# A fused transformer block: the second gate/up starts with twelve half tiles, one norm is transposed by DMA, and one chunk's Q, K, V become paired matmuls

## The chip, the cores and the metric

The kernel runs on one core of a Trainium2 chip. The metric is the device time of one execution in microseconds (us); the number compared is the median of several executions. The profile comes from one further execution that was taken with the hardware profiler.

## What is computed

The input x has 2048 rows of 576 values in bf16. A small matrix product of silu(c) with w_mod gives six vectors of 576: shift, scale and gate for each of two halves.

```python
h = layernorm(x) * (1 + ca) + sa
x = x + ga * attention(h)          # 32 heads of 18, each row attends to 8 rows: itself and 2, 4, .. 14 back
h = layernorm(x) * (1 + cb) + sb
x = x + gb * ((h @ w_gate) * (h @ w_up)) @ w_down      # 576 -> 4608 -> 576
```

## The kernel before

The rows are cut into eight chunks of 256 (two tiles of 128 rows each), and the chunks into five groups for the second half: [0], [1, 2], [3, 4], [5, 6], [7]. For each group the kernel runs a gate/up stage (`gate_up`: 36 column tiles of 128, each the product of gate and up) and then a down stage (`down`: 36 row tiles accumulated into PSUM). The attention of later chunks is cut into small pieces that are put between the tiles of these stages, so that TensorE always has matmuls to run.

The contraction over 576 is four and a half times 128. A *pair* (class `Pair`) runs two matmuls at once, one on rows 0 to 63 of the array and one on rows 64 to 127, so that the half step costs half; the tail of the operand must then be present in both halves of the partitions (`both` in the norms writes it twice, `both_halves` and `wo_both` copy it for the weights). The *full* form pads the half step to 128 rows. Before the change, chunks 0, 1, 2 and 4 use the full form for Q, K, V (`a_q`, `a_v`) and chunks 3, 5, 6 and 7 use pairs (`qkv_of`); the output projection is a pair for chunks 3, 5 and 7 (`wo_of`) and full for the others (`b_w`).

A normalised chunk must be transposed before it can be multiplied. Either TensorE does it through PSUM (`transposed`, used by `a_t` and `b_t`; the modulation then reads PSUM), or the DMA does it from SBUF to SBUF (`a_td`, `b_td`, issued on SP; the modulation `a_mod` or `b_mod` then works in place). `b_o` transposes the attention output o_sb to oT on TensorE, `b_od` by DMA.

**The order.** All engines run in the order in which the program issues instructions. `timed` makes that order: it walks the tiles of a stage with a clock of assumed costs, and after each tile takes pieces from several threads. A piece is a tuple (TensorE us, VectorE us, the marks it needs, the mark it makes, the wait until that mark counts, the call). Pairs come from a list of their own (`extra`), at most one before each tile, in order. What did not fit in a gate/up stage goes to the down stage behind it (`among`, `first_down`), and what did not fit there is the `left` of the next gate/up.

**The second gate/up** (group [1, 2]) can begin on chunk 1 alone: `gate_items` starts it with `HEAD` = 8 half tiles for chunk 1 ("f0", 256 columns), then the same 8 for chunk 2 ("f1", which need the mark h2), then whole tiles of 512 columns. Weights for gate and up (`load_wgu`, on SP) come in blocks of four tiles into three buffers, so block 3 can only be asked for when block 0 has been used by both chunks: at the fifth f1 tile. W_down (`load_wd`) and the values of attention (`b_ld`, 1.1 MB each) are loaded on GpSimd's queue.

**Chunk 2 before the change**: its values are weighted and summed in the first down stage, its output projected (`b_o`, `b_w`), its second norm (`b_ln`, `b_norm`) finished at the start of the second gate/up and transposed by TensorE there (`b_t(2)`). Chunk 4's norm is transposed by TensorE (`a_t4`) at the start of the first down stage, and its Q, K, V follow there in the full form. Chunk 1's output projection is there too.

Of the kernel before, what the change touches and what calls it, by code (L numbers as in the profile page):

```python
# [39 lines left out]
GC = D // 4  # L40

GROUPS = [[0], [1, 2], [3, 4], [5, 6], [7]]
PAIRED = (3, 5, 7)


@with_exitstack
def kernel(
# [279 lines left out]
    def transposed(src, dst, cols, vi):  # L327
        n = P * len(cols)
        pA = ps([P, 3, n], BF, "tr_pA")
        pB = ps([P, 2, n], BF, "tr_pB")  # L330
        for m in range(KT):
            d = pA[:, m, :] if m < 3 else pB[:, m - 3, :]
            for c, j in enumerate(cols):
                nc.tensor.transpose(d[:, js(c)], src[:, j, m * P:(m + 1) * P], ident[:])

        def evict(first_on_dve=True):
            for m in range(KT):
                s = pA[:, m, :] if m < 3 else pB[:, m - 3, :]
                modulate(dst(m), s, m, vi + 1, vi, (m < 3) == first_on_dve)
        return evict  # L340

    def mod_columns(wm, pi, fill=lambda: None, steps={}, order=(KF, 0, 1, 2, 3)):
# [49 lines left out]

    def a_ln(i):
        x = x_in.pop(i)
        xn, rsq, norm = layernorm(lambda j: x[:, j, :], "a", i in (3, 4), i in (3, 5, 6, 7))
        aa[i] = dict(xn=xn, rsq=rsq, norm=norm)

    def a_norm(i):
# [21 lines left out]
            nc.sync.dma_start_transpose(out=aa[i]["hT"][:, :, js(j)], in_=aa[i]["xn"][:, j, :])  # L420

    def a_t4():
        a_t(4, False)
        nc.gpsimd.memset(aa[4]["hT"][64:, KF, :], 0.0)

    def a_mod(i, ms, on_dve=True):
        hT = aa[i]["hT"]
# [47 lines left out]
    def b_ld(i, j):  # L475
        b = bb.setdefault(i, dict(prod={}, vsh={}))
        base = HALO + i * CH + j * P - DIL * (W - 1)
        vsh = vshp.tile([P, W, DH, H], BF, name="vsh")
        vsrc = bass.AP(vd.tensor, vd.offset + base * D, [[D, P], [DIL * D, W], [1, D]])
        b["vsh"][j] = vsh  # L480
        return nc.gpsimd.dma_start(vsh[:].rearrange("p w d h -> p w (d h)"), vsrc)  # L481

    def b_p(i, w):
        b = bb.setdefault(i, dict(prod={}, vsh={}))
# [197 lines left out]
        transposed(bb.pop(i)["xn"], lambda m: ht[:, m, o0:o0 + CH], (0, 1), 2)()  # L682


    def b_td(i):
        ht, o0 = h2_of(i)
        xn = bb.pop(i)["xn"]
        for j in range(ST):
            nc.sync.dma_start_transpose(out=ht[:, :, o0 + j * P:o0 + (j + 1) * P], in_=xn[:, j, :])

    def b_mod(i, ms, on_dve):
        ht, o0 = h2_of(i)
# [32 lines left out]
    def values_of(i, nxt=None):  # L725
        r = []
        for j in range(ST):
            r += [(0, 0.75, f"a{i}", "-", 0, lambda j=j, w=w: b_mul(i, j, w)) for w in range(0, W, 2)]
            r += [(0, 0.75, "", "-", 0, lambda j=j: b_add(i, j, 0)), (0, 0.75, "", "-", 0, lambda j=j: b_add(i, j, 1)),
                  (0, 1.2, "", f"o{i}{j}", 0, lambda j=j: b_add(i, j, 2))]  # L730
            if i in PAIRED:
                r.append((0, 0, "", f"O{i}" if j == ST - 1 else "-", 11.0 if i == 7 else 14.0, lambda j=j: b_od(i, (j,))))
            if nxt is not None:

                r.append((0, 0, f"v{nxt}", "-", 0, lambda j=j: behind(b_ld(nxt, j), bb[i]["od"]) if (i, j) == (3, 1) else b_ld(nxt, j)))
        return r
# [153 lines left out]

    QKP = [(0, 1), (2, 3), (4,), (5, 6), (7, 8)]

    def timed(items, extra, threads, slack, busy=0.0):

        t, dve = 0.0, busy
        done, seq = {f"v{i}": 0.0 for g in GROUPS for i in g[1:]}, []
        done["late"] = 0.0
        extra, threads = list(extra), [list(th) for th in threads]

        def ready(need):  # L900
            return all(done.get(x, 1e9) <= t for x in need.split())

        def fill():
            nonlocal t, dve
            moved = True
            while moved:
                moved = False
                for th in threads:
                    if th and ready(th[0][2]) and (not th[0][1] or dve <= t + slack):
                        pe, d, _, mark, wait, call = th.pop(0)  # L910
                        t += pe
                        dve = max(dve, t) + d if d else dve
                        done[mark] = (dve if d else t) + wait
                        seq.append(("piece", call))
                        moved = True
                        break
        for kind, f, step, own, need in items:
            if seq and extra and ready(extra[0][1]):
                pe, _, mark, make, *ve = extra.pop(0)
                seq.append(("pair", make))  # L920
                t += pe
                dve = max(dve, t) + sum(ve)
# [7 lines left out]
        assert not extra, (extra[0][1], t)  # L930
        return seq, [(*p[0:2], p[2] if all(x in names(th) for x in p[2].split()) else "late", *p[3:]) for th in threads for p in th]

    def names(th):
        return [p[3] for p in th]
# [7 lines left out]
                at[f].append(x)  # L942
        return at, late

    HEAD = 2 * FB

    def gate_items(gi):
        n = len(GROUPS[gi])
# [37 lines left out]
    def wgu_spaces():  # L986
        for k, space in ((3, value_space()), (4, value_space()), (8, prod_t)):
# [1 line left out]
        load_wgu((NG - 1) * NBLK + 3)  # L989
        load_wgu((NG - 1) * NBLK + 4)  # L990

    WD_ASKS = [{0: (7,), 1: (8,), 2: (9,), 7: (10,)},
# [339 lines left out]
    def ld_prods(gi):  # L1332
        for k in range(2):
            g = gi * NBLK + (5 if gi == 0 else 3) + k
            wd_home[g] = prod_t[:, k * FB * D:(k + 1) * FB * D].rearrange("p (k d) -> p k d", d=D)
            r = load_wd(g)
            if gi:
                behind(r, wgu_in[gi * NBLK + NBLK - 1])

    loads = {(0, 23): lambda: behind(load_wd(1), bb[2]["ltd"]), (0, 24): lambda: ld_d1(4), (0, 25): lambda: load_wd(2), **{(gi, 32): lambda gi=gi: ld_prods(gi) for gi in (1, 2, 3)}, (3, 34): wgu_spaces, (NG - 1, 28): lambda: [ld_spare(k) for k in range(4)]}  # L1340

# [18 lines left out]
    at = [k for k, p in enumerate(first) if p[3] == "o11"][0] + 2  # L1360
    first.insert(at, (0, 0, "o11", "O1", 0, nop))
    gbg = {0: (qkv_of(3, "p17 z3"),
               [[(0, 0, "", "-", 0, lambda: (load_wm5(), load_wd(0))), (0, 0, "", "z3", 8.0, nop), (0, 0, "", "w5", 12.0, nop), (0.85, 0, "w5", "-", 0, gb_row), (0, 0, "", "-", 0, lambda: (load_res(2), both_halves()))],
                norm_of(3, "", "", 5) + [(0, 2.5, "", "m4", 0.2, lambda: a_ln(4)), (0, 0, "m4", "r4", 1.0, lambda: aa[4]["rsq"]()),
                                         (0, 0, "r4", "e4", 2.0, lambda: aa[4]["norm"]((0,))), (0, 0, "e4", "n4", 1.6, lambda: aa[4]["norm"]((1,))),
                                         (0, 0, "n4 v3", "x4", 0, nop)],
               first, [(0, 0, "y1", "s1", 0.6, lambda: b_exp(1))]]),
           1: (qkv_of(5, "p37") + wo_of(3),
               [[(0, 0, "", "-", 0, lambda: (loads_v(3), load_res(3), load_res(4), wo_both()))], norm_of(5, "p33", "", 7), second]),
           2: (qkv_of(6, "") + wo_of(5),  # L1370
               [[(0, 0, "", "h6", 1.0, lambda: (loads_v(5), load_res(5), load_res(6)))], attention_of(5, 6)]),
           3: (qkv_of(7, "") + wo_of(7), [[(0, 0, "", "h7", 1.0, lambda: load_res(7)), (0, 0, "v7", "-", 0, lambda: loads_v(7))], [(0, 0, "q74", "-", 0, nop)] + prods_of(7) + softmax_of(7) + values_of(7)]),
           4: ([], [])}

    def first_down(late):
        def q(g):
            return (0.53 if g == 2 else 1.07, 0, "h4", "-", 0, lambda: a_q(4, g))

        def v(j):
            return (1.2, 0, "h4", "-", 0, lambda: a_v(4, j))  # L1380

        def out_1(first):
            return [(0, 0, "", "o0", 0.4, nop), (0.55, 0, "o0", "o1", 1.9, lambda: b_o(1)), (1.2, 1.35, "o1", "-", 0, lambda: b_w(1, 0)), (1.2, 1.35, "", "x1", 0.5, lambda: b_w(1, 1)),
                    (0, 2.5, "", "s1", 0.7, lambda: b_ln(1)), (0, 0, "s1", "n1", 2.3, lambda: b_norm(1)), (0, 0, "n1", "t1", 9.5, lambda: b_td(1)),
                    (0, 1.0, "t1", "-", 0, lambda: (b_mod(1, (3, 4), False), b_mod(1, (0, 1, 2), True)))]
        assert not {"O1", "x4"} & set(names(late))
        a4 = [(0.6, 0, "", "h4", 1.7, lambda: (a_t4(), load_x(6), ld_prods(0)))]
# [19 lines left out]
    for gi, grp in enumerate(GROUPS):  # L1407
# [13 lines left out]
        if gi == NG - 1:  # L1421
            down_last(gi, hh)
        else:
            left = down(gi, hh, first_down(late) if gi == 0 else next_down(gi, late))
            assert gi == 0 or not left


# [28 lines left out]
```

## Time and profile before

| | us |
|---|---|
| three executions | 539.7, 540.89, 541.5 (median 540.89) |
| the profiled execution | 541.99 |
| its span, first to last instruction | 539.7 |
| first gate/up (49.3 to 95.8) | 46.5 |
| first down (95.8 to 127.6) | 31.8 |
| second gate/up (127.6 to 210.1) | 82.5 |

In those three stages TensorE is busy for 46.45, 31.49 and 82.50 us, VectorE for 38.6, 22.8 and 64.7, ScalarE for 34.7, 14.0 and 48.0. The granted TensorE clock is 1.00 throughout. PE is TensorE, DVE VectorE, ACT ScalarE, POOL GpSimd, SP the engine that issues most DMAs. In a group of instructions, "x25" is their number; in a timeline the first two columns are start and duration, and brackets hold the idle time before the instruction and what ended it.

### The profile page before, as it was taken

Reading aid. Unit: us, or ns where it says so; the run is one execution under the profiler, and the core shown is the slowest. Engines: PE = TensorE matmul, PEld = TensorE weight load, DVE = VectorE, ACT = ScalarE, POOL = GpSimd, SP = SyncE. Lnnn points to the kernel's source line nnn. Section 1 sums busy time; section 2 is a strip of 40 time slices with the busy share of each in tenths; the row PEclk is TensorE's granted clock in tenths of the full one; section 3 lists DMA queues with packets and bytes.
Section 4 is the critical chain, followed back from the end, with each engine's and each line's share of the span. In section 5 each row is a group of like instructions: output and inputs, shape, how many; then the busy total and the mean of one; then the engine's idle time right before and its main releaser. Section 6 shows DMA issues by size and latency. Waiting matters only on the chain.

```text
span 539.7 us, 14692 instructions
## 1 busy us (share of the span) xinstructions
PE 531.5 (98%) x6214; PEld 324.0 (60%) x6244; DVE 319.5 (59%) x731; ACT 252.8 (47%) x620; POOL 73.1 (14%) x113
## 2 busy tenths in 40 slices
PE   8999999999999999999999999999999999999997
PEld 4777889756755444555544454555544454558875
DVE  5898797759767788627467797504517733032212
ACT  4866877644656553112655543104555542006630
POOL 8104023112000110111000010110010101110210
PEclk9999999999999999999999999999999999999999
DMA  9999999979863871998445944983396694759731
GB/s 273 292 242 363 346 278 321 322 128 326 279 181 90 237 229 28 264 273 299 130 130 145 302 149 108 238 237 111 94 279 184 158 312 81 233 138 292 259 96 38
DMA packets 94659, 114.47 MB, mean 212 GB/s; under 512 B 27873, under 2 KB 83378, under 8 KB 94466
## 3 DMA queue, kind: packets, MB, share of 16 engines
q1 hardware_dynamic: 82864, 66.92, 45.7%
q0 software_dynamic: 11424, 46.40, 27.5%
q8 instruction: 49, 0.80, 0.7%
q10 hardware_dynamic: 306, 0.21, 0.1%
q14 instruction: 16, 0.13, 0.1%
HBM read 103.07 MB, written 4.74 MB: 200 GB/s over the span
## 4 chain that ended last, share of the span: by engine, by line
PE 97%; DMA 1%; issue 1%; DVE 0%; SPq 0%; ACT 0%
PE pg L770 29%; PE pu L770 23%; PE acc L1007 19%; PE pq L442 4%; PE pq L770 3%; PE accr L1012 3%; PE acc L1062 3%; PE pv L770 2%; PE pv L465 2%; PE lgT L499 2%; PE pw L659 2%; DMA wmA<-in_w_mod_dram 1%; PE pw L770 1%; PE po L614 1%; PE pwj L636 0%
## 5 line engine op out<-in xcount | busy, mean ns | idle before, releaser
L770 PE MATMUL pg<-h2T,wgu 64*128 64x512 bf16 (+1 forms) x1376 | 266.0, 331 | 0.0
L770 PE MATMUL pu<-h2T,wgu 64*128 64x512 bf16 (+1 forms) x1376 | 265.5, 331 | 0.0
L770 PEld LDWEIGHTS <-wgu 64*128 64x128 bf16 x2752 | 136.5, 94 | 93.3
L821 ACT CAST u_sb<-pu 128x512 bf16<-128x512 f32 (+1 forms) x172 | 85.4, 497 | 152.4 <-PE pg L770 150.4
L824 DVE TENSOR_TENSOR hh<-g_sb,u_sb 128x512 bf16<-128x512 bf16 x136 | 59.2, 435 | 114.1 <-ACT g_sb L822 113.1
L822 ACT CAST g_sb<-pg 128x512 bf16<-128x512 f32 (+1 forms) x172 | 86.8, 505 | 0.0
L1007 PEld LDWEIGHTS <-hh 128*128 128x128 bf16 x504 | 49.0, 98 | 59.3 <-issue 1.5
L1007 PE MATMUL acc<-wd,hh 128*128 128x512 bf16 x327 | 84.1, 380 | 0.1
L1012 PE MATMUL accr<-wd,hh 128*128 128x64 bf16 x344 | 62.4, 193 | 0.8
L770 PE MATMUL pu<-h2T,wgr 64*128 64x512 bf16 (+1 forms) x188 | 61.4, 327 | 0.0
L770 PE MATMUL pg<-h2T,wgr 64*128 64x512 bf16 (+1 forms) x188 | 61.4, 327 | 0.0
L1012 PEld LDWEIGHTS <-hh 128*128 128x128 bf16 x504 | 45.8, 98 | 1.2
L175 POOL DMA_DIRECT2D wd<-in_B_w_down_dram x29 | 21.8, 751 | 176.2 <-PE accr L1012 142.0
L548 DVE TENSOR_TENSOR vsh<-vsh,attn 128x1152 bf16<-128x1152 bf16 x56 | 39.7, 750 | 0.0
L487 DVE TENSOR_TENSOR prod_t<-qT,kT 128x1280 bf16<-128x1280 bf16 x36 | 28.2, 817 | 4.5 <-ACT kT L841 2.7
L770 PEld LDWEIGHTS <-wgr 64*128 64x128 bf16 x376 | 19.6, 94 | 15.1 <-issue 2.7
L1007 PE MATMUL acc<-prod_t,hh 128*128 128x512 bf16 x108 | 27.7, 380 | 0.0
L481 POOL DMA_DIRECT2D vsh<-vd x14 | 12.5, 896 | 96.6 <-DVE o_sb L556 76.1
L770 PE MATMUL pq<-hT,wqk 64*128 64x256 bf16 (+1 forms) x360 | 22.9, 259 | 0.0
L442 PE MATMUL pq<-hT,wqk 128*128 128x256 bf16 (+1 forms) x225 | 21.7, 251 | 0.1
L1012 PE MATMUL accr<-prod_t,hh 128*128 128x64 bf16 x112 | 21.6, 193 | 0.2
L325 ACT ACTIVATE h2T<-h2T,modc 128x256 bf16<-128x256 bf16 x12 | 6.5, 591 | 31.4 <-DMA h2T<-xn 31.4
(225 smaller groups left out, 628.3 us busy)
## 6 DMA issues: line engine op xcount, KB each, us to landing
wgu<-in_B_w_gate_dram SPq DMA_DIRECT2D x41, 512.0 KB, 4.8
wgu<-in_B_w_up_dram SPq DMA_DIRECT2D x41, 512.0 KB, 6.5
wd<-in_B_w_down_dram POOLq DMA_DIRECT2D x29, 576.0 KB, 5.2
vsh<-vd POOLq DMA_DIRECT2D x14, 1152.0 KB, 8.8
prod_t<-in_B_w_down_dram POOLq DMA_DIRECT2D x8, 576.0 KB, 5.9
hh<-in_B_w_down_dram POOLq DMA_DIRECT2D x6, 576.0 KB, 6.8
x_t<-in_A_x_dram SPq DMA_DIRECT2D x8, 288.0 KB, 5.3
x_r<-in_A_x_dram SPq DMA_DIRECT2D x8, 288.0 KB, 8.5
```

The lines of the kernel that those rows point to most:

```text
L175: return nc.gpsimd.dma_start(wb[:], B_w_down[r0:r0 + FB * P, :].rearrange("(k p) n -> p k n", p=P))
L442: nc.tensor.matmul(pq[:, gi, :], lhsT=wqk[:, kt, m * P:(m + 1) * P], rhs=hT[:, kt, cols], start=(kt == order[0] and not (by_k and gi)), st ...
L481: return nc.gpsimd.dma_start(vsh[:].rearrange("p w d h -> p w (d h)"), vsrc)
L487: nc.vector.tensor_tensor(prod, aa[i]["qT"][:], aa[i]["kT"][:, :, off:off + CH], ALU.mult)
L548: nc.vector.tensor_tensor(v, v, at, ALU.mult)
L770: return nc.tensor.matmul(out, lhsT=lhs, rhs=rhs, start=first, stop=last, skip_group_check=True)
L821: nc.scalar.copy(u[:, c, :], pu)
L822: nc.scalar.copy(g[:, c, :], pg)
L824: return lambda: nc.vector.tensor_tensor(hh[:, f - c:f + 1, :], g, u, ALU.mult)
L1007: nc.tensor.matmul(acc[j][:], lhsT=hh[:, f, js(j)], rhs=wb[:, f % FB, 0:512], start=(f == 0), stop=(f == FT - 1))
L1012: nc.tensor.matmul(accr[:, j, :], lhsT=hh[:, f, js(j)], rhs=wb[:, f % FB, 512:D], start=(f == 0 and j == 0), stop=(f == FT - 1), skip_grou ...
L1062: nc.tensor.matmul(acc[i][:], lhsT=hh[:, f, js(j)], rhs=wb(f)[:, c0:c1], start=(f == 0), stop=(f == FT - 1))
```

## The change

- `HEAD` becomes 12: the second gate/up begins with twelve half tiles of chunk 1, then twelve of chunk 2.
- Chunk 2's second norm is transposed by DMA (`b_td(2)` and `b_mod(2, ..)` in place of `b_t(2)`). The reads of chunk 3's values wait until that transpose has landed and until h2 in the program; the residual loads of chunks 3 and 4 move with them in the program's order.
- Chunk 4's Q, K, V become pairs: the five for Q and K at the end of the first gate/up, the two for V at the start of the second. Its norm writes its tail twice; its transposes on TensorE move from the first down stage into the first gate/up, and their eviction is all on VectorE. The load of chunk 6's input moves with them.
- Chunk 1's output projection becomes two pairs in the first gate/up; `b_o(1)` moves there, its tail columns of o_sb are filled, and `wo_both` is issued earlier. Chunk 1's second norm is modulated by VectorE alone.
- Chunk 2's weighted values are held back in the planner until 52.5 and 56.5 on its clock (marks V2 and W2).
- `timed` may place pairs after the last tile. W_down's loads in the first down stage are asked for at other tiles, and blocks 5 and 6 wait for chunk 2's first value read.

```diff
-PAIRED = (3, 5, 7)
+PAIRED = (1, 3, 5, 7)
...
-                modulate(dst(m), s, m, vi + 1, vi, (m < 3) == first_on_dve)
+                modulate(dst(m), s, m, vi + 1, vi, first_on_dve == 5 or (m < 3) == first_on_dve)
...
-        xn, rsq, norm = layernorm(lambda j: x[:, j, :], "a", i in (3, 4), i in (3, 5, 6, 7))
+        xn, rsq, norm = layernorm(lambda j: x[:, j, :], "a", i in (3, 4), i >= 3)
...
     def a_t4():
-        a_t(4, False)
-        nc.gpsimd.memset(aa[4]["hT"][64:, KF, :], 0.0)
+        a_t(4, 5)
+        load_x(6)
...
-            if i in PAIRED:
+            if i in PAIRED[1:]:
...
+        for pe, need, mark, make, *_ in extra:
+            assert ready(need), (need, t)
+            seq.append(("pair", make))
+            t += pe
+            done[mark] = t + pe + 1.0
+            fill()
...
-    HEAD = 2 * FB
+    HEAD = 3 * FB
...
-    WD_ASKS = [{0: (7,), 1: (8,), 2: (9,), 7: (10,)},
+    WD_ASKS = [{0: (7,), 3: (8,), 5: (9,), 7: (10,)},
...
-            if gi:
-                behind(r, wgu_in[gi * NBLK + NBLK - 1])
+            behind(r, wgu_in[gi * NBLK + NBLK - 1] if gi else bb[2]["ld"])
...
-    first = attention_of(1, 2)[12:-14]
+    first = attention_of(1, 2)[12:]
+    first.insert(-14, (0, 0, "V2", "-", 0, nop))
+    first.insert(-7, (0, 0, "W2", "-", 0, nop))
...
-    gbg = {0: (qkv_of(3, "p17 z3"),
+    gbg = {0: (qkv_of(3, "p17 z3") + wo_of(1) + qkv_of(4, "p27")[:5],
...
+               [(0, 2.5, "W11", "S1", 0.7, lambda: b_ln(1)), (0, 0, "S1", "N1", 2.3, lambda: b_norm(1)), (0, 0, "N1", "T1", 9.5, lambda: b_td(1)),
+                       (0, 1.7, "T1", "-", 0, lambda: b_mod(1, (3, 4, 0, 1, 2), True))],
+               first, [(1.15, 0, "o11 n4 v3", "O1", 2.3, lambda: (a_t4(), b_o(1))), (0, 0, "O1", "h4", 0.6, nop)],
+               [(0, 0, "y1", "s1", 0.6, lambda: b_exp(1))], [(0, 0, "", "V2", 52.5, nop)], [(0, 0, "", "W2", 56.5, nop)]]),
-           1: (qkv_of(5, "p37") + wo_of(3),
-               [[(0, 0, "", "-", 0, lambda: (loads_v(3), load_res(3), load_res(4), wo_both()))], norm_of(5, "p33", "", 7), second]),
+           1: (qkv_of(4, "")[5:] + qkv_of(5, "p37") + wo_of(3),
+               [[(0, 0, "", "h4", 0, nop), (0, 0, "h2", "-", 0, lambda: (load_res(3), load_res(4), behind(b_ld(3, 0), tds[2]), b_ld(3, 1)))], norm_of(5, "p33 M2", "v4", 7), second]),
...
-              (0, 2.2, "", "s2", 0.7, lambda: b_ln(2)), (0, 1.5, "s2", "n2", 0.2, lambda: b_norm(2)), (0.55, 1.0, "n2", "-", 0, lambda: b_t(2))]
-        return [a4, out_1(True), late + [(0, 0, "", "a2", 0.0, nop)] + values_of(2) + o2, [q(0), q(1), q(2), q(3), q(4), v(0), v(1)]]
+              (0, 2.2, "", "s2", 0.7, lambda: b_ln(2)), (0, 1.5, "s2", "n2", 0.2, lambda: b_norm(2)), (0, 0, "n2", "T2", 6.0, lambda: b_td(2)),
+              (0, 0, "T2", "M2", 0, lambda: (b_mod(2, (3, 4), False), b_mod(2, (0, 1, 2), True)))]
+        return [[(0, 0, "", "-", 0, lambda: ld_prods(0))]] + parts[:-1] + [parts[-1] + o2]
```

More of the change, by code (lines that the diff above doesn't have):

```diff
@@ L480, in b_ld @@
         b["vsh"][j] = vsh
-        return nc.gpsimd.dma_start(vsh[:].rearrange("p w d h -> p w (d h)"), vsrc)
+        r = nc.gpsimd.dma_start(vsh[:].rearrange("p w d h -> p w (d h)"), vsrc)
+        b.setdefault("ld", r)
+        return r
     def b_p(i, w):
@@ L682, in b_t @@
         transposed(bb.pop(i)["xn"], lambda m: ht[:, m, o0:o0 + CH], (0, 1), 2)()
+    tds = {}
     def b_td(i):
@@ L688, in b_td @@
         for j in range(ST):
-            nc.sync.dma_start_transpose(out=ht[:, :, o0 + j * P:o0 + (j + 1) * P], in_=xn[:, j, :])
+            tds[i] = nc.sync.dma_start_transpose(out=ht[:, :, o0 + j * P:o0 + (j + 1) * P], in_=xn[:, j, :])
     def b_mod(i, ms, on_dve):
@@ L891 @@
     QKP = [(0, 1), (2, 3), (4,), (5, 6), (7, 8)]
+    parts = []
     def timed(items, extra, threads, slack, busy=0.0):
@@ L897, in timed @@
         done["late"] = 0.0
+        for x in extra:
+            done.pop(x[2], None)
         extra, threads = list(extra), [list(th) for th in threads]
@@ L929, in timed @@
             t += step
-        assert not extra, (extra[0][1], t)
-        return seq, [(*p[0:2], p[2] if all(x in names(th) for x in p[2].split()) else "late", *p[3:]) for th in threads for p in th]
+        for pe, need, mark, make, *_ in extra:
[4 more added lines that the diff above has]
+            fill()
+        parts[:] = [[(*p[0:2], p[2] if all(x in names(th) for x in p[2].split()) else "late", *p[3:]) for p in th] for th in threads]
+        return seq, [p for th in parts for p in th]
     def names(th):
@@ L1359 @@
     first.pop(at)
-    at = [k for k, p in enumerate(first) if p[3] == "o11"][0] + 2
-    first.insert(at, (0, 0, "o11", "O1", 0, nop))
-    gbg = {0: (qkv_of(3, "p17 z3"),
-               [[(0, 0, "", "-", 0, lambda: (load_wm5(), load_wd(0))), (0, 0, "", "z3", 8.0, nop), (0, 0, "", "w5", 12.0, nop), (0.85, 0, "w5", "-", 0, gb_row), (0, 0, "", "-", 0, lambda: (load_res(2), both_halves()))],
+    gbg = {0: (qkv_of(3, "p17 z3") + wo_of(1) + qkv_of(4, "p27")[:5],
+               [[(0, 0, "", "-", 0, lambda: (load_wm5(), load_wd(0))), (0, 0, "", "z3", 8.0, nop), (0, 0, "", "w5", 12.0, nop), (0.85, 0, "w5", "-", 0, gb_row), (0, 0, "", "-", 0, lambda: (load_res(2), both_halves(), wo_both()))],
                 norm_of(3, "", "", 5) + [(0, 2.5, "", "m4", 0.2, lambda: a_ln(4)), (0, 0, "m4", "r4", 1.0, lambda: aa[4]["rsq"]()),
-                                         (0, 0, "r4", "e4", 2.0, lambda: aa[4]["norm"]((0,))), (0, 0, "e4", "n4", 1.6, lambda: aa[4]["norm"]((1,))),
-                                         (0, 0, "n4 v3", "x4", 0, nop)],
-               first, [(0, 0, "y1", "s1", 0.6, lambda: b_exp(1))]]),
-           1: (qkv_of(5, "p37") + wo_of(3),
-               [[(0, 0, "", "-", 0, lambda: (loads_v(3), load_res(3), load_res(4), wo_both()))], norm_of(5, "p33", "", 7), second]),
+                                         (0, 0, "r4", "e4", 2.0, lambda: aa[4]["norm"]((0,))), (0, 0, "e4", "n4", 1.6, lambda: aa[4]["norm"]((1,)))],
+               [(0, 2.5, "W11", "S1", 0.7, lambda: b_ln(1)), (0, 0, "S1", "N1", 2.3, lambda: b_norm(1)), (0, 0, "N1", "T1", 9.5, lambda: b_td(1)),
[4 more added lines that the diff above has]
+               [[(0, 0, "", "h4", 0, nop), (0, 0, "h2", "-", 0, lambda: (load_res(3), load_res(4), behind(b_ld(3, 0), tds[2]), b_ld(3, 1)))], norm_of(5, "p33 M2", "v4", 7), second]),
            2: (qkv_of(6, "") + wo_of(5),
@@ L1373, with first_down @@
            4: ([], [])}
[L1375 to L1387, printed above, removed]
+    def first_down(parts):
         o2 = [(0, 0, "o21", "z2", 0.6, nop), (0.55, 0, "z2", "O2", 1.1, lambda: b_o(2)), (1.2, 1.35, "O2", "-", 0, lambda: b_w(2, 0)), (1.2, 1.35, "", "x2", 0.2, lambda: b_w(2, 1)),
-              (0, 2.2, "", "s2", 0.7, lambda: b_ln(2)), (0, 1.5, "s2", "n2", 0.2, lambda: b_norm(2)), (0.55, 1.0, "n2", "-", 0, lambda: b_t(2))]
-        return [a4, out_1(True), late + [(0, 0, "", "a2", 0.0, nop)] + values_of(2) + o2, [q(0), q(1), q(2), q(3), q(4), v(0), v(1)]]
+              (0, 2.2, "", "s2", 0.7, lambda: b_ln(2)), (0, 1.5, "s2", "n2", 0.2, lambda: b_norm(2)), (0, 0, "n2", "T2", 6.0, lambda: b_td(2)),
+              (0, 0, "T2", "M2", 0, lambda: (b_mod(2, (3, 4), False), b_mod(2, (0, 1, 2), True)))]
+        return [[(0, 0, "", "-", 0, lambda: ld_prods(0))]] + parts[:-1] + [parts[-1] + o2]
     def norm2_of(i, need):
@@ L1423 @@
         else:
-            left = down(gi, hh, first_down(late) if gi == 0 else next_down(gi, late))
+            left = down(gi, hh, first_down([th for k, th in enumerate(parts) if th and k != 3] + [parts[3]]) if gi == 0 else next_down(gi, late))
             assert gi == 0 or not left
```

## The prediction

> **What bounds the kernel now.** I read the page first, then the waits of the engines, then TensorE's timeline around the edits. The page's busy shares and its chain agree:
>
> ```profile
> span 539.7 us, 14692 instructions
> ...
> PE 531.5 (98%) x6214; PEld 324.0 (60%) x6244; DVE 319.5 (59%) x731; ACT 252.8 (47%) x620; POOL 73.1 (14%) x113
> ...
> PE 97%; DMA 1%; issue 1%; DVE 0%; SPq 0%; ACT 0%
> ```
>
> The chain that ended last is TensorE for 97% of the span. All of TensorE's waits in the whole run, from the view of waits:
>
> ```profile
> PE busy L203 <- DVE busy_w L198: 1.3, 1, 1.3
> PE pv L465 <- issue: 1.1, 1, 1.1
> PE pm L348 <- DMA wmA<-in_w_mod_dram: 0.5, 1, 0.5
> PE pm_t L355 <- PE pm L348: 0.2, 1, 0.2
> ```
>
> All four lie in the prologue, before the first gate/up. (Matmul ends are modelled, so I also compared starts: apart from steps where one record is missing, they show some 1.05 us of delay after 49 us, 0.88 of it at chunk 3's Q, which the change leaves in place.) So the edits are worth the TensorE time that they remove, less any wait that they make. Removed work can bring little; a new wait can cost without limit.
>
> **The change, part by part.** TensorE first, from its timeline:
>
> ```profile
> 103.65 2.89 PE L442 MATMUL pq<-hT,wqk 128*128 128x256 bf16 x25
> 106.38 1.23 PE L465 MATMUL pv<-wv,hT 128*128 128x504 bf16 x5
> 107.44 0.33 PE L467 MATMUL pvr<-wv,hT 128*128 128x72 bf16 x5
> 107.60 1.23 PE L465 MATMUL pv<-wv,hT 128*128 128x504 bf16 x5
> ...
> 132.19 0.51 PE L334 MATMUL tr_pA<-shifts,xn 128*128 128x128 bf16 x6
> 132.54 0.39 PE L334 MATMUL tr_pB<-shifts,xn 128*128 128x128 bf16 x4
> 132.86 0.28 PE L770 MATMUL pg<-h2T,wgr 64*128 64x256 bf16 x1
> ```
>
> and from the chain, pieces of the paired form (chunk 5, chunk 3) beside the full form:
>
> ```profile
> 100.41 1.08 PE pw L659 x5
> ...
> 160.81 0.98 PE pq L770 x18
> ...
> 176.34 1.10 PE pv L770 x18
> ...
> 199.91 1.10 PE pw L770 x18
> ```
>
> Ends overlap the next start, so I take start to start.
>
> 1. *Chunk 4's Q, K, V as pairs.* Now: Q and K are 45 matmuls at 2.73/25 = 0.109 us, 4.91; V is 106.38 to 108.82, 2.44 (the next start). Together 7.35. As pairs: four at 0.98, the half-width one 0.50, two V pairs at 1.10: 6.62. Gain 0.73.
> 2. *Chunk 1's output projection as pairs.* Now 1.08 + 0.15 to 0.21 per tile, 2.51 for two; then 2 x 1.10 = 2.20. Gain 0.31.
> 3. *Chunk 2's second norm by DMA.* Ten transposes leave TensorE: 132.19 to 132.86, 0.67.
> 4. *Twelve half tiles.* Four more tiles cost 2 x 0.982 in place of 1.942 (pitch of half and of full tiles in this stage): +0.09.
> 5. *Chunk 4's and chunk 1's transposes* move from the down stage into the first gate/up. There a change between 64-row and 128-row matmuls costs 0.09 going in and 0.10 coming out (the last half-tile start at 131.99 to 132.19 is 0.20 where the pitch is 0.11): +0.19.
>
> Sum: -0.73 - 0.31 - 0.67 + 0.09 + 0.19 = -1.43 us.
>
> The small edits off TensorE I cost at nothing while TensorE covers them: two more 64-column normalisations on ScalarE for chunk 4, tail adds and memsets of o_sb on VectorE, five modulations moved from ScalarE to VectorE (0.34 each), the copy of wo's tail moved earlier on GpSimd, the memset of hT removed there. VectorE and ScalarE are busy 39 and 35 of 46.5 us in that gate/up; with the cover gone they cost their own 1 to 2 us. The moved loads of W_down I cost at nothing too: blocks 5 and 6 now follow chunk 2's first value read (landed at 97.5), take about 6 us and are needed at down tile 20, 10 us into a stage that starts at 103.8; blocks 7 and 8 start when blocks 0 and 1 are used up, 12 us or more before their tiles, and loads here took 5 to 10. Chunk 6's input is asked a few places earlier on SP and needed far later.
>
> **The waits that it adds.** I walked the planner's rule with the new costs to get the order, and put measured durations on it. The order is unchanged up to tile 32 of the first gate/up (92.4 us). That stage then gains 7.9 us (0.56 + 0.56 + 0.19 + 2.20 + 4.42) and ends at 103.8 instead of 95.85; the first down stage loses 11.0 (7.35 + 2.51 + 2 x 0.56) and ends at 124.6 instead of 127.6.
>
> *PSUM after the moved transposes.* Four banks go through 20 transposes in the middle of the gate tiles; VectorE must drain chunk 4's (5 x 0.34 = 1.7 us, behind the softmax of chunk 2) before two tiles later uses them. Bounds 0 and 0.9; I take 0.2, since the drained banks are due only 1.1 us after the transposes end, about when the first three are drained.
>
> *Chunk 1's transpose and VectorE.* It is issued at about 109, and all five modulations now stand in VectorE's queue ahead of chunk 2's two residual sums, its statistics, and the output of the down stage, which frees the accumulators. How long it takes to land, from the view of tile h2T and the group by line:
>
> ```profile
> L689 SPq DMA_TRANSPOSE h2T<-xn x2: 1200/1251/1302, 111.6 to 112.9; - x2
> ...
> DMA to landing us min/median/max: 7.6/8.9/10.2
> ```
>
> Landing at 119, modulated at 120.5; sums 2.7, statistics 2.0, first accumulators read by 126.9. TensorE asks for those banks at about 127.4. Margin 0.5 us; bounds 0 and 2; I take 0.2.
>
> *Chunk 2's transpose.* Output rows end near 128.3, the normalisation (1.63) at 130, the second DMA is issued near 131. The other transposes onto h2T took 4.9 to 10.3 us, median 6.4: 137.2, with modulation 138.3. The twelve first halves, V4's two pairs and chunk 3's logits (1.3) put TensorE at the second halves at 124.6 + 11.8 + 2.2 + 1.3 = 139.9. Bounds 0 and 2.4 (10.3 instead of 6.4); I take 0, because chunk 3's value reads, the traffic beside the present transposes, now wait for it.
> The Trainium skill ("VectorE: DVE Perf Modes", Rules for kernel authors) says to use TensorE for a 128x128 transpose where a PSUM destination will do, and the DMA crossbar otherwise. By that rule item 3 would be left out, and the sum would be -0.76. Here the page and the rows agree on latency (0.67 us against several), but TensorE's time is what this kernel is short of.
>
> *Weight block 3 of the second gate/up.* With twelve half tiles its buffer is still freed at second half 4, and it is needed at tile 12, but SP's queue now has chunk 3's logit transposes and chunk 5's transposes (which wait for its normalisation, about 142.9) ahead of it. Now:
>
> ```profile
> 140.96 0.37 SPq L158 DMA_DIRECT2D wgu<-in_B_w_gate_dram  x1
> 141.37 0.51 SPq L158 DMA_DIRECT2D wgu<-in_B_w_up_dram  x1
> ...
> 146.46 2.60 SPq L420 DMA_TRANSPOSE hT<-xn  x2
> 149.11 0.59 SPq L140 DMA_DIRECT2D x_t<-in_A_x_dram  x1
> ```
>
> Afterwards the order is reversed, and the asks move to about 146.6 and 147.1. Loads here land in 3.9 to 6.5 us: 151.1 to 153.6. TensorE is at tile 12 at 152.1 (139.9 + 0.4 + 11.8). Bounds 0 and 1.5 in that range, more if the value reads still fill the engines; I take 0.4.
>
> So -1.43 + 0.2 + 0.2 + 0.4 = -0.6 us. Span 539.7 becomes 539.1; the profiled execution (541.99, 2.3 outside the span) 541.4. That execution is 1.1 above the median of the runs, so on the median: 540.89 - 0.6 = 540.3.
>
> **Rivals.**
> - *No new wait*: all margins hold; 540.89 - 1.43 = 539.5, 0.26% faster. For it: each wait above is under 0.5 us as worked out, and the present trace has none of them. Against: three margins of about half a microsecond must all hold. Chance 0.28.
> - *More than the sum*: the 1.05 us of delays at chunk 3's Q shrink with the new bank order, 538.6. Against: nothing moves ahead of that place. Chance 0.08.
> - *Slower: weight block 3 comes late.* SP waits for chunk 5's norm with the block's two loads queued behind it, and those then share the DMA engines with 2.4 MB of chunk 3's values, which were let go only at about 137. The four wgu loads asked between 114 and 117 landed 10 to 12 us after their ask in such traffic. At 8.5 us the block lands at 155.6, TensorE waits 3.5, and the time is 540.89 - 1.43 + 3.5 + 0.4 = 543.4; at 12 it is 547. It decides (over 0.3% slower) from a landing after 154.8, 7.7 us after the ask. Chance 0.15.
> - *The transposes by DMA are too slow for the edit*: 10.3 us for chunk 2's second one gives 2.4 us at the second halves, plus 0.4: 542.3. The same chain is late if chunk 1's lands at 122. For: the two transposes of this very stage took 7.6 and 10.2. Against: the traffic beside them has moved. Chance 0.12. The Trainium skill's rule on transposes, above, points this way.
> - *The change does not do what it says*: the pairs and the order are written out, so the instructions will be there. I give it nothing.
>
> **How the numbers follow.** A difference of 0.3% (1.6 us) is about what a measurement of this kernel can tell from none. The forecast (0.37) gives no difference in 0.30, faster in 0.05, slower in 0.02. "No new wait" lies just inside the bound, half and half: 0.14 faster, 0.14 same. "More" is faster (0.08). Late weights: slower 0.14, same 0.01. Late transposes: at 542.3 and later, slower 0.08, same 0.04. Faster 0.27, same 0.49, slower 0.24. The forecast's own range is 539.7 to 541.2. The whole range reaches below the full gain by the scatter of the runs (539.5 - 0.8), and above it to 543.0, which takes in late transposes and the near end of late weights.
>
> **What would show it.** TensorE's busy time must fall by about 1.4 us; pq L442 loses 45 matmuls of 256 columns and L334 ten transposes. Right: h2T by DMA lands before 138, wgu for tile 12 lands near 152, and TensorE's new waits add to under 1.5 us. Wrong: a gap at the first second half with the DMA h2T as its releaser, one at tile 12 released by wgu, or VectorE idle for over 4 us before chunk 1's modulation with TensorE then waiting for accumulators.

## The result: 1.2 us slower, and two waits that explain it

The median after the change is 541.78 us (540.15 to 544.21, 22 executions), before it 540.57 us (539.22 to 542.5, 22 executions beside them). The ratio is 1.0024, with a 95% interval of 1.0014 to 1.0033. The forecast was 0.6 us faster; the kernel became 1.2 us slower. 541.78 lies inside the range that was given, but not inside the forecast's own.

I compare the two profiled executions stage by stage, from TensorE's start in a stage to its start in the next. The parts ahead of the first gate/up differ by 1.45 us between the two executions (the stage starts at 49.31 before and at 47.86 after) although the change touches nothing there, so the spans (539.7 and 539.8) hide what happened. It also means that 1.45 us must be added to a time in the changed profile before it is set beside a time that the prediction names.

| stage, us | before | forecast | after |
|---|---|---|---|
| first gate/up | 46.54 | 54.5 | 54.85 |
| first down | 31.76 | 20.8 | 20.76 |
| second gate/up | 82.45 | 84.9 | 86.76 |
| the three together | 160.75 | 160.15 | 162.37 |
| all the rest, to the last matmul | 325.87 | as before | 325.85 |

(The forecast's third row is the sum of -0.6 less the first two.) The first down stage came out to a tenth of a microsecond. The loss is in the second gate/up, with 0.35 us in the first.

The page of the changed kernel:

```profile
span 539.8 us, 15006 instructions
...
PE 530.7 (98%) x6355; PEld 328.7 (61%) x6383; DVE 320.5 (59%) x746; ACT 252.4 (47%) x631; POOL 72.9 (14%) x112
```

TensorE's busy time fell from 531.5 to 530.7 us, in the direction of the sum but by 0.8 instead of 1.4; since the ends of matmuls are modelled, I rely on their starts. The profiled execution took 541.75 us, the span and 1.95 around it. The view of TensorE's waits (us in total, times, longest) has three rows for these stages, where the kernel before had none:

```profile
PE pg L774 <- ACT u_sb L817: 1.2, 1, 1.2
PE pu L774 <- DMA wgu<-in_B_w_up_dram: 0.9, 1, 0.9
PE pq L774 <- ACT qT L843: 0.3, 1, 0.3
```

By matmul starts they are 1.49 us (two steps, at 150.48 and 150.75), 1.06 us at 153.13, and 0.43 us at 78.76 where the kernel before lost 0.09. Another 0.10 us stands after the moved transposes at 93.58. So 1.49 + 1.06 + 0.34 + 0.10 = 2.99 us of new waits; the three stages grew by 1.62; the work itself changed by 1.62 - 2.99 = -1.37 us, where the sum had -1.43. (These are two single executions; the medians differ by 1.21 us.)

**The first wait.** A matmul waits for a PSUM bank that ScalarE should have drained (u_sb L817 is the cast out of the bank). ScalarE's timeline shows why it had not:

```profile
146.67 0.38 ACT L818 CAST g_sb<-pg 128x256 bf16<-128x256 f32 x1
149.54 0.63 ACT L522 ACTIVATE dd<-dd 128x512 f32<-128x512 f32 x1 [2.48 <-DVE dd L530]
```

L522 is the exponential of chunk 3's softmax (`b_exp`, called by `b_sm0`). It stands in ScalarE's queue ahead of the next casts and waits 2.48 us for VectorE's difference. VectorE's timeline has the link behind it:

```profile
147.76 1.02 DVE L529 TENSOR_REDUCE mx<-lg_t 128x64 f32<-128x512 bf16 x1 [1.36 <-DMA lg_t<-lgs]
```

The maximum waits for chunk 3's logits, which a DMA transposes (`b_ltd`, lg_t). The view of that tile in the changed kernel gives its latency:

```profile
DMA to landing us min/median/max: 7.3/7.8/8.3
```

The planner allows 6.0 us for this step, and before the change it took 3.9 to 4.9:

```profile
DMA to landing us min/median/max: 3.9/4.4/4.9
```

So the chain is: transpose late, VectorE late, ScalarE's queue blocked, banks not drained, TensorE idle.

**The second wait** is weight block 3 of the second gate/up, as forecast. SP's timeline:

```profile
139.15 2.48 SPq L519 DMA_TRANSPOSE lg_t<-lgs  x2
141.74 2.53 SPq L420 DMA_TRANSPOSE hT<-xn  x2
144.32 0.57 SPq L140 DMA_DIRECT2D x_t<-in_A_x_dram  x1
144.99 1.89 SPq L158 DMA_DIRECT2D wgu<-in_B_w_gate_dram  x1
146.93 0.50 SPq L158 DMA_DIRECT2D wgu<-in_B_w_up_dram  x1
```

Chunk 5's transposes (L420) are now ahead of the block's two loads, which land at 151.61 and 153.09. TensorE reaches tile 12 at 151.64 and needs the up half at 152.07.

### The profile page after: what moved, and what is told of

Same layout as the page of the kernel before. It is cut to its first block, busy times and chain, and to the rows that moved or that the text cites. A ratio compares the mean times of both kernels' runs of the same rounds, so it can differ in the third digit from the quotient of the medians.

```text
span 539.8 us, 15006 instructions
## 1 busy us (share of the span) xinstructions
PE 530.7 (98%) x6355; PEld 328.7 (61%) x6383; DVE 320.5 (59%) x746; ACT 252.4 (47%) x631; POOL 72.9 (14%) x112
## 4 chain that ended last, share of the span: by engine, by line
PE 95%; DVE 1%; DMA 1%; issue 1%; ACT 1%; SPq 0%
PE pg L774 28%; PE pu L774 23%; PE acc L1021 19%; PE pq L774 4%; PE accr L1026 3%; PE pq L442 3%; PE acc L1076 3%; PE pv L774 2%; PE pw L774 2%; PE lgT L501 1%; PE pv L465 1%; PE pw L661 1%; DMA wgu<-in_B_w_up_dram 1%; PE busy L203 1%; PE po L616 1%
## 5 line engine op out<-in xcount | busy, mean ns | idle before, releaser
L774 PEld LDWEIGHTS <-wgu 64*128 64x128 bf16 x2816 | 140.5, 94 | 92.0 <-DMA wgu<-in_B_w_up_dram 1.4
L825 ACT CAST u_sb<-pu 128x512 bf16<-128x512 f32 (+1 forms) x168 | 83.4, 496 | 154.4 <-PE pg L774 149.5
L828 DVE TENSOR_TENSOR hh<-g_sb,u_sb 128x512 bf16<-128x512 bf16 x132 | 57.4, 435 | 110.9 <-ACT g_sb L826 109.9
L826 ACT CAST g_sb<-pg 128x512 bf16<-128x512 f32 (+1 forms) x168 | 84.7, 504 | 0.0
L774 PE MATMUL pg<-h2T,wgr 64*128 64x256 bf16 (+1 forms) x192 | 62.1, 323 | 1.2 <-ACT u_sb L817 1.2
L774 PE MATMUL pu<-h2T,wgr 64*128 64x256 bf16 (+1 forms) x192 | 62.1, 323 | 0.0
L774 PE MATMUL pq<-hT,wqk 64*128 64x256 bf16 (+1 forms) x450 | 28.4, 258 | 0.3 <-ACT qT L843 0.3
L774 PEld LDWEIGHTS <-wqk 64*128 64x128 bf16 x450 | 22.3, 94 | 5.9 <-issue 1.0
L1049 DVE TENSOR_TENSOR t_r<-accr,gb_bc 128x256 bf16<-128x256 f32 (+1 forms) x4 | 1.5, 378 | 39.2 <-PE accr L1026 39.2
```

The source lines that it names most:

```text
L774: return nc.tensor.matmul(out, lhsT=lhs, rhs=rhs, start=first, stop=last, skip_group_check=True)
L825: nc.scalar.copy(u[:, c, :], pu)
L826: nc.scalar.copy(g[:, c, :], pg)
L828: return lambda: nc.vector.tensor_tensor(hh[:, f - c:f + 1, :], g, u, ALU.mult)
```

## The experiments

The times of one group of runs stand beside the kernel before on the same chip. In the first group its median is 540.59 us, in the second 540.44, in the third 540.60. Between groups the ratios are the better comparison.

### The exponential later

```diff
-  ... 9.0 if i == 7 else 6.0, lambda: [b_ltd(i, w) for w in (0, 4)])]
+  ... 9.0 if i in (3, 7) else 6.0, lambda: [b_ltd(i, w) for w in (0, 4)])]
-  (0, 0, f"n{n} {free}", f"x{n}", 8.0, go)
+  (0, 0, f"n{n} {free}", f"x{n}", 10.5 if n == 5 else 8.0, go)
```

> Chunk 3's maximum, difference and exponential are put three half tiles later (the planner allows 9.0 us instead of 6.0 for its logit transposes, and 10.5 instead of 8.0 for chunk 5's). Theory 'in series': the 1.49 us in which ScalarE's exponential held up the casts at 150.5 goes, but TensorE then reaches tile 12 at 150.1 instead of 151.6, while weight block 3 still lands at about 153.1; its wait there grows from 1.06 to about 2.5 us and the time stays within 0.2 us of 541.8. Theory 'each counts': the gap of 1.49 us goes and the wait for the block stays at 1.06: 540.3. Theory 'neither': the loss lies elsewhere, 541.8 with the block's wait unchanged at 1.06.

Measured: 541.83 us, ratio to before 1.0035 (1.0017 to 1.0054). TensorE's waits in the second gate/up:

```profile
PE pu L774 <- DMA wgu<-in_B_w_up_dram: 1.1, 1, 1.1
PE pg L774 <- DMA wgu<-in_B_w_gate_dram: 0.5, 1, 0.5
```

The wait for ScalarE is gone and the time did not move. The wait for the block grew from 1.06 to 1.96 us by starts (0.68 for the gate half, 1.28 for the up half), and the second gate/up shrank by only 0.60 us in the profile. The two waits stand one behind the other: of the 1.49 us, 0.90 came back as a longer wait for the block. "Each counts" falls, since the median did not move; "in series" fits, though it had put the block's wait at 2.5 us. The block's wait alone, 1.96 us, is more than the 1.43 us that the change saves.

### The weight block first

```diff
- norm_of(5, "p33 M2", "v4", 7), second]
+ norm_of(5, "p33 M2", "v4 K5", 7), second, [(0, 0, "h2", "K5", 8.0, nop)]]
```

with the 10.5 us for chunk 5's transposes, as above.

> Weight block 3 of the second gate/up is asked ahead of chunk 5's transposes on SP's queue (their step is held back by 8.0 us of the planner's time after chunk 2's halves are ready). 'In series' and 'each counts' both say: the block is asked at about 143.2 and 143.7, lands before 150.5, the wait of 1.06 us at tile 12 goes and the ScalarE wait of 1.49 stays: 540.7. 'Neither': 541.8. If chunk 5's transposes now land after its modulation stands in VectorE's queue, up to 1 us comes back as late casts near 153.

Measured: 540.11 us, ratio 0.9998 (0.9984 to 1.0012): the loss is gone. The gain is larger than expected, because no new wait of TensorE is left in the second gate/up: the ScalarE wait went too. That stage takes 84.11 us, and 82.45 plus the work alone (2.20 for the two V pairs, 0.09, -0.67) is 84.07. The reason is in the tile of the logits:

```profile
DMA to landing us min/median/max: 4.6/5.4/6.2
```

Chunk 5's transposes are now issued 3.4 us behind the second of the logits' instead of 1.4, with the block's loads in between (asked at 143.81 and 144.22, landed by 150.27). The logits land at 146.0 instead of 147.7. That is enough: the exponential waits 1.03 us instead of 2.48, and the banks are drained in time. My expectation missed that one reordering would mend both waits.

### Both edits

The two edits together.

> Both edits together. 'In series': the ScalarE wait and the wait for block 3 both go, 1.49 + 1.06 = 2.55 us, 539.2, which is 1.3 us under the kernel before, as the sum of TensorE's work says. 'Each counts' gives the same 539.2 here; it differs in the first of these kernels. 'Neither': 541.8. Between: 539.2 to 540.2 if chunk 5's transposes, now later, make VectorE wait.

Measured: 540.13 us, ratio 0.9993 (0.9982 to 1.0004), the same as the block first alone. There was nothing left for the first edit to remove, so the expected 539.2 was 0.9 too low. In the profile the second gate/up takes 83.98 us, 2.78 less than after the change, while the medians differ by 1.65. A profile is one execution: this one lost 0.56 us more in the first gate/up (55.41 us; see the copies below), and the stretch ahead of that stage, which no edit touches, differs by up to 1.8 us between the profiles.

### Chunk 3's value reads early

```diff
- [(0, 0, "", "h4", 0, nop), (0, 0, "h2", "-", 0, lambda: (load_res(3), load_res(4), behind(b_ld(3, 0), tds[2]), b_ld(3, 1)))]
+ [(0, 0, "", "h4", 0, lambda: loads_v(3)), (0, 0, "h2", "-", 0, lambda: (load_res(3), load_res(4)))]
```

> Chunk 3's two value reads (1.2 MB each) are issued at the start of the second gate/up and no longer behind chunk 2's transposes; the rest is the changed kernel. Theory 'shared engines': the logit transposes land 7 to 8 us after their issue because these reads run beside them; with the reads done by about 139 they land within 5.5 us, at 144.5, the ScalarE wait of 1.49 us goes and the block's up half lands nearer 151.5, wait at tile 12 near 1.0 to 1.4: 540.3 to 540.6. Theory 'own queue': the transposes are slow because three pairs of loads follow each other on SP within 6 us; they still take over 7 us and the time stays at 541.8. In both, chunk 2's transposes lose their free stretch and land later than 133.8; over 137 they would hold TensorE at the second halves.

Measured: 545.67 us, ratio 1.0095 (1.0079 to 1.0112). The logits' transposes, with the reads done by 139.6, now take 2.3 us from issue to landing although chunk 5's transposes still follow 1.3 us behind:

```profile
DMA to landing us min/median/max: 2.3/2.3/2.3
```

So "shared engines" holds and "own queue" falls: what follows on SP's queue counts, as with the block first, only while the reads run. But chunk 2's transposes, now beside the reads, took 12.0 and 11.0 us instead of 5.6 and 5.4 and landed at 141.5. ScalarE's timeline:

```profile
141.58 1.09 ACT L325 ACTIVATE h2T<-h2T,modc 128x256 bf16<-128x256 bf16 x2 [4.83 <-DMA h2T<-xn]
```

Its part of the modulation stood ahead of the casts of the first halves, and TensorE lost 4.1 us before chunk 3's logits. It is the same mechanism at another transpose. I had named 137 as the limit, but had not priced what lies behind it. There is a second cost: shortly after this wait the granted TensorE clock is 0.50 for 3.4 us (the third number from the end), and TensorE is busy for all of them:

```profile
144.20:147.60 3.40, 3.40 (x38) 2.45 (x36) 2.41 (x11) 2.18 (x7) 0.00 (x0) 0.50 0.10 22
```

At half the clock this stretch does 1.7 us less work (an estimate). 4.1 and 1.7 are 5.8 of the 6.0 us by which this second gate/up (90.09 us) is longer than the one without waits (84.11). Holding the reads behind chunk 2's transposes, as the change does, is worth 3.9 us between the medians.

### The reads behind the logits

The two reads are issued right behind chunk 3's logit transposes and wait for them.

```diff
+ second.insert(10, (0, 0, "", "-", 0, lambda: (behind(b_ld(3, 0), bb[3]["ltd"]), b_ld(3, 1))))
- ... lambda: (load_res(3), load_res(4), behind(b_ld(3, 0), tds[2]), b_ld(3, 1)))]
+ ... lambda: (load_res(3), load_res(4)))]
```

> The changed kernel with chunk 3's two value reads put behind its logit transposes, everything else in place. 'The reads make the logits late': the logit transposes land 2.3 to 4 us after their issue, by 144.5, with chunk 5's transposes still right behind them, and the ScalarE wait of 1.49 us goes. The reads then run beside weight block 3, which still takes 6 to 8 us from its ask (gate at 145.0, up between 145.5 and 146.9), lands at 151.5 to 153.5 and makes TensorE wait 1.4 to 3 us from 150.1: about 541.2, between 540.7 and 542.2. 'Chunk 5's transposes make the logits late': the logit transposes still take over 6.5 us, the ScalarE wait stays, 541.8 or more.

Measured: 551.4 us, ratio 1.0193 (1.0175 to 1.021). The first half of the expectation holds: the logits took 2.3 and 4.3 us and the ScalarE wait is gone. The second is far off. TensorE's timeline at tile 12:

```profile
158.84 0.60 PE L774 MATMUL pg<-h2T,wgu 64*128 64x512 bf16 x1 [8.05 <-DMA wgu<-in_B_w_gate_dram]
```

The block was asked at 146.28 and 146.75, within 1.4 us of the reads (145.42 and 146.32), and landed 12.5 and 13.6 us later. I had priced it at 6 to 8 us, the latency beside reads that were half done; two loads of 512 KB that start behind 2.3 MB of reads wait for nearly all of it. This is the prediction's rival of the late block, at its full price and more: the second gate/up takes 96.64 us, 12.5 more than without waits, and TensorE's two waits for the block are 9.3 of them by starts. The rest is the clock, which is 0.50 from 155.8, 5 us after TensorE ran dry, to 166.1, 7.2 us after it went on; at half speed this costs about 3 us (an estimate):

```profile
155.90:166.00 10.10, 6.25 (x37) 2.89 (x39) 2.40 (x4) 1.32 (x5) 0.00 (x0) 0.50 0.71 222
```

The Trainium skill ("DMA: Bandwidth & Descriptors", Queues, rings and completion order) says that each engine takes turns between the queues that have work. By turns of equal bytes the block's 1 MB would land long before the last read, but here the gate half landed 0.4 us after the second read. The view of the DMA from 150 to 156 us shows why (packets, MB, share of the engines; q0 is GpSimd's queue with the reads, q1 is SP's):

```profile
q0 software_dynamic: 393, 1.70, 79.7%
q1 hardware_dynamic: 424, 0.43, 22.8%
```

The two queues moved nearly the same number of packets, which agrees with taking turns, but a packet of the reads carried 4.3 KB and one of SP's queue 1.0 KB.

### Chunk 2's second norm on TensorE again

From the kernel with the block first:

```diff
- (0, 0, "n2", "T2", 6.0, lambda: b_td(2)), (0, 0, "T2", "M2", 0, lambda: (b_mod(2, (3, 4), False), b_mod(2, (0, 1, 2), True)))
+ (0.55, 1.0, "n2", "M2", 0, lambda: b_t(2))
- behind(b_ld(3, 0), tds[2]), b_ld(3, 1)
+ loads_v(3)
```

> The kernel with weight block 3 first, and chunk 2's second norm transposed on TensorE again (ten transposes) in place of the DMA; chunk 3's reads then have nothing to wait for but chunk 2's buffers. By the prediction's third term the ten transposes put 0.67 us back on TensorE: 540.8 against 540.1. If the DMA transposes cost as much somewhere else (the rule that TensorE is the path to take), it is 540.1 or less. Above 541.1 a new wait would have come with the earlier order of VectorE and SP.

Measured: 540.87 us against 540.11; the ratio to before is 1.0005 (0.9996 to 1.0014). In the profile the second gate/up takes 84.85 instead of 84.11 us, 0.74 more, about the 0.67 us of the ten transposes. The third term of the sum (0.67) is right by that stage, which took 83.98 to 84.12 us in four profiles with the DMA transposes and no new wait; the medians alone would not show it, since the two ratios' intervals overlap. The rule of the Trainium skill ("VectorE: DVE Perf Modes", Rules for kernel authors) that TensorE is the path to take loses here by these 0.7 us: the DMA transposes' 5 us landed inside the first halves and cost nothing.

### Chunk 4's normalisation later

From the kernel with the block first:

```diff
- (0, 0, "m4", "r4", 1.0, lambda: aa[4]["rsq"]())
+ (0, 0, "m4", "r4", 6.0, lambda: aa[4]["rsq"]())
```

> The kernel with weight block 3 first, and chunk 4's normalisation on ScalarE put 5 us of the planner's time later, past chunk 3's Q pairs. Theory 'ScalarE's extra columns': the two normalisations of chunk 4 grew from 0.89 to 1.22 us because of the 64 doubled columns, and stand on ScalarE just before the casts that free chunk 3's Q banks; the gap near 79 us falls from 0.43 to 0.1 us or less, the first gate/up takes 54.5 us instead of 54.8, and the time is 539.8. Rival 'bank order': the gap comes from the pairs' own banks and stays at 0.43: 540.1.

Measured: 539.68 us, ratio 0.999 (0.9976 to 1.0004). The gap near 79 us is gone altogether. In the changed kernel this line stands just ahead of the casts that free chunk 3's Q banks:

```profile
77.22 1.22 ACT L308 ACTIVATE xn<-x_t,ln_nbt,ln_rstda 128x576 bf16<-128x576 bf16 x2
```

Before the change the same normalisation stood at the same place in ScalarE's queue without the doubled columns, and the gap was 0.09 us:

```profile
78.87 0.89 ACT L308 ACTIVATE xn<-x_t,ln_nbt,ln_rstda 128x576 bf16<-128x576 bf16 x1
```

So it was the doubled columns, 0.33 us of ScalarE's time, that made the difference. But the first gate/up of this profile took 55.13 us, not 54.5: there is 0.42 us at chunk 3's first Q pair (73.05) and 0.21 near 69. Four profiles of other variants have the first gap too (0.3 to 0.6 us). VectorE's timeline, and GpSimd's:

```profile
70.12 3.89 DVE L323 TENSOR_SCALAR hT<-hT,modc 128x256 bf16<-128x256 bf16 x5
```

```profile
70.53 1.17 POOL L1339 COPY wqk<-wqk 64x1152 bf16<-64x1152 bf16 x1
71.62 0.69 POOL L1339 COPY wv<-wv 64x576 bf16<-64x576 bf16 x1
72.23 0.68 POOL L875 COPY wo<-wo 64x576 bf16<-64x576 bf16 x1
```

Five modulations of 0.34 us take 3.89; the first alone is 2.87 us long and ends at 72.99, when the last copy ends (72.91). The third copy is the one that the change moved here. The median is 0.43 us under that of the block first alone, but the intervals overlap and this profile shows no gain in the stage.

### The copies moved

From that kernel, first the copy of wo's tail behind chunk 4's normalisation:

```diff
- ... lambda: (load_res(2), both_halves(), wo_both()))],
+ ... lambda: (load_res(2), both_halves()))],
+ [(0, 0, "n4", "-", 0, wo_both)],
```

> The kernel with block 3 first and chunk 4's normalisation late, with one more change on GpSimd's queue: the copy of wo's tail (0.7 to 0.9 us) comes after chunk 4's normalisation, near 88 us, and no longer right behind the copies of wqk's and wv's tails at 72. Theory 'the copies hold VectorE': in several profiles a VectorE instruction beside these copies takes 1.9 to 2.9 us instead of 0.34 to 0.42 and ends with the last copy, so chunk 3's modulation ends late and its first Q pair waits 0.2 to 0.5 us near 73. Without the third copy VectorE is free 0.7 us earlier, that gap goes, and the first gate/up takes 54.5 us instead of 55.1; time 539.4, 0.3 under 539.7. Rival 'the transpose lands late': the gap follows the landing of chunk 3's transposes (68.1 to 69.1) and stays: 539.7.

Measured: 539.28 us, ratio 0.997 (0.9951 to 0.9989). This is the lowest median, 2.5 us under that of the changed kernel, and the only version whose interval lies wholly under the kernel before; it overlaps those of the last kernel and of the next. In the profile the first gate/up takes 54.71 us. Chunk 3's five modulations take 3.16 us instead of 3.89, shorter by the missing copy (0.7 us), and the first ends with the copy of wqk's tail. The gap at the first Q pair is 0.15 us at most, although chunk 3's transposes landed late in this execution (69.9); so it does not follow the landing. A step of 0.5 us near 69.4, whose releaser the profile does not name, is still there.

Then both other copies at the start of that stage too (`both_halves()` ahead of `load_wm5()`):

> As the kernel before this one, and the copies of wqk's and wv's tails are issued at the start of the first gate/up, near 50 us, instead of 70. 'The copies hold VectorE': chunk 3's five modulations take 1.7 us and no instruction of VectorE near 70 takes over 0.9 us; the gap near 73 is gone in every profile; 539.3. The hold of some 1.9 us moves to 50 to 60 us, where VectorE has slack in the order of 1 us a tile; if it has not, up to 0.5 us appears there. 'The transpose lands late': the gap near 73 stays, 539.7.

Measured: 539.76 us, ratio 0.9982 (0.9963 to 1.0001), no gain over the one move. The modulations near 71 are short again (1.37 us for five) and the gap near 73 is gone. The hold went along with the copies: at 50.5 one product takes 1.76 us instead of 0.82, the copies themselves take 1.67 and 1.26 instead of 1.17 and 0.70, and TensorE shows 0.41 us at 52.3 and 0.3 more than the other variants at 58.9. So the copies do hold VectorE. Whether moving them pays stays open: this first gate/up took 54.52 us, 0.19 less than with the one move, and the second 84.47, 0.35 more, because the logits landed at 146.57 and the exponential waited 1.4 us again. The Trainium skill ("SBUF — State Buffer", SBUF: two separate sides) calls this an exclusive lock on a port pair that VectorE and GpSimd share; the 2.87 us that end with the last copy agree with it.

## Why the prediction was wrong

- **TensorE's terms (-1.43 us): right.** After the change the stages give -1.37 once the waits are taken off, and the variant without waits in the second gate/up has 84.11 us there against 84.07 from the terms. The term for chunk 2's transposes was tested by itself (0.74 against 0.67); those for the pairs only as part of the sum. The first down stage lost exactly the 11.0 us.
- **"The waits that it adds": this step failed.** It counted SP's logit transposes only as things ahead of the block's loads. They are themselves moved, from behind the block (issued at 149.8 before) to in front of it (139.2 after), while the change puts chunk 3's value reads off from 128.7 to 134.4; so the two meet, and I never priced the transposes' landing: 7.3 to 8.3 us. Everything that hangs on it was missing: VectorE's maximum, the exponential on ScalarE, the casts queued behind it, and the banks. That wait is 1.49 us, and no rival named it.
- **The block's wait: right mechanism, wrong size.** I took 0.4 and measured 1.06, inside the bounds of 0 to 1.5. But those bounds were too narrow: with the other wait gone it is 1.96 us, by itself more than the 1.43 us saved. The landing was mis-sized: with the 1.45 us by which this execution starts earlier, the two loads were asked at 146.4 and 148.4 (forecast 146.6 and 147.1), took 6.6 and 6.2 us, and landed at 153.1 and 154.5 (forecast 151.1 to 153.6). The second ask was late because the issue of the first took 1.89 us on SP where it had taken 0.37. TensorE's own way was right: it began the second halves at 139.8 on that clock, forecast 139.9, and was at tile 12 at 153.1, 1.0 after the forecast, because of the first wait.
- **"Costed at nothing": one item wrong.** Chunk 4's two 64-column normalisations cost 0.34 us at chunk 3's Q, where I had looked only at ScalarE's share of busy time and not at what stands behind them in its queue. Moving them from that place took the gap away in the profile; what it is worth in the median (0.43 us) is not clear of the noise. The copy of wo's tail lengthened chunk 3's modulations by 0.7 us in one profile and the stage there by about 0.4, also through the order of a queue that I had counted as free; the medians do not prove this either.
- **PSUM after the moved transposes, chunk 1's and chunk 2's DMA transposes:** 0.10, 0 and 0 us, against 0.2, 0.2 and 0. Chunk 1's landed at 118.0 instead of 119, chunk 2's at 135.2 instead of 137.2, with the 1.45 us added.
- **The rivals.** The late block decided from a landing after 154.8 us; it landed at 154.5 (153.09 + 1.45), so that rival just failed to happen as priced, though its sign, a gap at tile 12 released by the block, is there. "Too slow transposes" named the right kind of cause but the wrong transposes. In the sum: 0.8 us of waits forecast, 2.99 measured.

The reordered versions give back what the change lost. The sum of TensorE's work alone would give 540.57 - 1.43 = 539.14, and the lowest median is 539.28; in its profile the three stages take 159.59 us, 1.16 less than before.

## What to carry to other kernels

When an edit moves an instruction past another in a queue, price the landing of every DMA in the new order, and follow each late one through all queues behind it: here a transpose that landed 1.7 us too late reached TensorE over VectorE, ScalarE and a PSUM bank. Two waits that follow each other on one engine don't add up: removing one alone can give nothing, and a single move that mends the cause of both gives all. Where an engine works in order, its idle share says nothing about a 0.3 us addition; look at what stands right behind it.

## What was unexpected in the hardware's behaviour

- The same pair of small DMA transposes (128 KB together) took 2.3 us each with nothing large beside it, 4.6 to 6.5 us beside two reads of 1152 KB, and 6.1 to 8.3 us where chunk 5's transposes followed 1.4 us behind as well.
- Two loads of 512 KB asked right behind those reads, on another queue, took 12.5 and 13.6 us.
- In the two variants where TensorE stood for 4.0 us and longer at a stretch, its granted clock fell to 0.50, for 3.4 and 10.2 us; beside the waits of up to 1.5 us in the other profiles it stayed at 1.00 through these stages.
- Copies on GpSimd stretched one VectorE instruction from 0.34 to 2.87 us, and were themselves stretched from 1.17 to 1.67 us beside VectorE's products.
- A step of 0.2 to 0.5 us near 69 us shows in the profiles of four variants and not in others of the same code up to that point. In each of the four, the trace has a 16 KB packet on the DMA queue that the page calls "instruction" that ended 1.3 to 1.5 us before the late matmul, 19.6 to 19.9 us into the stage; in six of the seven without a clear step the last one had ended by 18.8 us. That TensorE waited for its instructions fits this, but no run varies it, so the cause stays open.
